# Reordering the opening loads and stores, the woven tiles' weight split and one prefix product in a fused spectral and expert kernel

## The chip, the cores and the metric

One core of one Trainium2 chip runs the whole program. The metric is the device time of one execution in microseconds. Three timed runs of the kernel before gave 1442.25 to 1444.67 us, with a median of 1443.52 us.

## What is computed

The input `x` has 8 batches of 2496 rows by 256 columns. Each batch is Fourier-transformed along its rows, mixed by a complex 256 by 256 weight, shrunk towards zero, and transformed back. Each of the 19968 rows then goes to the one of eight experts that its gate prefers.

```python
X = np.fft.rfft(x, axis=1)
Yr = Xr @ w_r - Xi @ w_i + b_r
Yi = Xr @ w_i + Xi @ w_r + b_i
Yr = np.sign(Yr) * np.maximum(np.abs(Yr) - 0.01, 0.0)
...
y = np.fft.irfft(Y, n=x.shape[1], axis=1)
...
logits = x @ w_gate
expert_idx = np.argmax(logits, axis=1)
...
h = np.maximum(xe @ w1[e], 0.0)
out[mask] = gate_w[mask, None] * (h @ w2[e])
```

## The kernel before, in words

The transform of 2496 = 39 x 64 points goes in two steps. The first (`fwd_a`, L367) multiplies the 39-point part and takes the input in six blocks per batch, `x(b, 0)` to `x(b, 5)`: five blocks of 117 rows (468 KB) and a last one of 78 rows (156 KB). `load_x` (L328) fetches a block. A block holds two pairs of columns `g = 0, 2`, the last one only `g = 0`, so a batch has eleven pairs and eleven products. What `fwd_a` makes is copied from PSUM to SBUF (`ae`, or for batch 0 the still unused tile `zs[1]`) and stored to a scratch tensor in HBM, `spec`, of 120 rows. The second step reads `spec` back, turned: `turn(b, s)` (L396) issues two loads of 128 KB each for slot `s` of ten slots, and slot `s` needs rows 12s to 12s+11 of all that was stored. I write t(n) for slot n counted over all batches, so t(10) is batch 1, slot 0.

For batches after the first, `round_x` (L356) makes on ScalarE (ACT) the rounded copy `xah` of a pair, and `rest_x` on GpSimd (POOL) makes its remainder. From batch 2 on `round_x` runs two iterations ahead of the product.

`spectral` (L582) is one order written by hand for TensorE (PE), VectorE (DVE), ACT and the DMA queue of SyncE (SP). After an opening for batch 0 alone it runs 80 iterations `it`, one per slot. Iteration `it` begins on PE with `fwd_b` of t(it+1), the products `pb` from `t` and the basis `bm`; then come `inv_b` (`pv`) of an earlier slot, `mix` (`pk`, `pm`), the `fwd_a` products of the next batch (`first`), and pieces of the batch before. ACT and DVE cut `pb` into `sh` and `sl` (`halves`, L420). `pb` has one PSUM buffer, so the next `fwd_b` waits until DVE's last read of it (`sl`, L430). At an iteration's end stand, in this order, `round_x` for two iterations on, the loads of the basis, the turns for five (at first) or four iterations on, and the loads of x blocks (`loads`).

SP issues its DMAs strictly in this order. A turn waits on SP until the stores of its rows have landed, and all that stands behind it on SP waits too. Basis `bm` comes in five pieces of 256 KB (`load_basis`); of the inverse basis `bi` three pieces are made by PE transposes and an ACT copy (`turn_basis`, L262), and two are loaded (`load_inverse`).

When the last batch has been transformed back, `finish_last` (L792) weaves the first seven expert tiles with the rest of the routing: after each step of a tile, `breathe` advances the queue of routing jobs. A tile t is `up` (hidden layer, products `ph`, L1137) and `down` (products `po`). Between the four quarters of `up`, `split2` (L1110) cuts the second half of a new expert's weights into `h2` under an `If` that holds only where the expert changes, and `upright` (L1119) prepares the next tile: a transpose, the rounding `xh` on ACT, the remainder `xl` on DVE. `route` (L833) yields "hold" ahead of its prefix product `pr` (L873), which keeps `tick` from going on until the next `breathe`.

Of the kernel before, what the change touches and what calls it, by code (L numbers as in the profile page):

```python
# [24 lines left out]
D = 256  # L25
# [84 lines left out]
class Kernel:  # L110
# [80 lines left out]
    def open_forward(self, st):  # L191
        tc, nc, nb = self.tc, self.nc, self.nb
        f = self.f = self.pool(st, "f", 1, side="right")
        self.xst = ExitStack()
        self.xp = self.pool(self.xst, "xp", 3)
        self.skip(self.xp, 224)
        self.xh, self.xl = {}, {}
        self.tp = self.pool(st, "tp", 6, side="right")
        self.w = self.pool(st, "w", 2, side="right")
        self.psf = self.pool(st, "psf", 1, side="right", space=PSUM)  # L200

        y = [self.w.tile([128, 2, D], F32, tag="y", name=f"first{i}", bufs=3) for i in range(2)]
        self.idle, self.row1, self.brow = y[0][:, 0, :].bitcast(BF16), y[0][0:1, 1, 0:128], y[1][0:1]
        nc.vector.memset(self.idle, 0.0)
        nc.vector.memset(self.row1, 1.0)
        far = f.tile([117, 240], F32, name="far")
        self.far, self.fer = far[:, 0:120], far[0:78, 120:240]
        nc.sync.dma_start(far, self.c_fa)
        self.bm = f.tile([128, K1, 128], F32, name="bm")
        self.bi = f.tile([128, K1, 128], F32, name="bi")  # L210
        self.bias = f.tile([128, 2, D], F32, name="bias")
        self.bias_r = f.tile([128, 2, D], F32R, name="bias_r")
        self.ones = f.tile([128, 128], F32R, name="ones")
        self.xg = {}
        for z, zf in zip(self.zs, self.zf):
            for c in range(2):
                nc.vector.memset(z[:, c, 64:66, :], 0.0)
            nc.vector.memset(zf[:, 5280:5288], 0.0)
        for q in range(6):
            self.load_x(0, q)  # L220
        raw = self.wi.tile([128, 4, D], F32, tag="yb", name="wraw", bufs=4)
        nc.sync.dma_start(raw, self.w_in.rearrange("(c p) n -> p c n", p=128))
        self.skip(self.wi, 160)
        self.raw = {"r": raw[:, 0:2, :], "i": raw[:, 2:4, :]}
        nc.sync.dma_start(self.brow, self.b_in.rearrange("(o h) n -> o h n", o=1))
        self.wh, self.wl = {}, {}
        for nm in "rds":
            self.wh[nm] = f.tile([128, 2, D], F32R, name="wh" + nm)
            self.wl[nm] = f.tile([128, 2, D], F32R, name="wl" + nm)
        self.nlam = f.tile([128, 1], F32, name="nlam")  # L230
        nc.vector.memset(self.nlam, -LAM)
# [138 lines left out]
    def fwd_a(self, b, q, g):  # L370
        nc = self.nc
        x = self.part_x(b, q, g)
        p = self.psi.tile([128, 512], F32, tag="u", name="pa", bufs=4)
        if b:
            h, l = self.xh.pop((b, q, g)), self.xl.pop((b, q, g))
            fh, fl = self.fhl[q == 5]
            for i, (a, v) in enumerate(((fh, h), (fl, h), (fh, l))):
                nc.tensor.matmul(p[:120, :], a, v, start=i == 0, stop=i == 2)
        else:
            nc.tensor.matmul(p[:120, :], (self.far if q < 5 else self.fer)[:x.shape[0], :], x, start=True, stop=True)  # L380
        n = 2 * q + g // 2 - 1
        if b or n < 0:
            ae = self.xp.tile([120, 2, D], F32, tag="ae", name="ae", bufs=4)
            to = ae.rearrange("p g d -> p (g d)")
        else:
            to = self.zs[1][:120, n // 5, 0:NB, :].rearrange("p n a -> p (n a)")[:, n % 5 * 512:n % 5 * 512 + 512]
            ae = to.rearrange("p (g d) -> p g d", g=2)
        if b == 0 and g:
            nc.vector.tensor_copy(to, p[:120, :])
        else:  # L390
            with self.tc.high_priority():
                nc.scalar.copy(to, p[:120, :])
        if b:
            nc.sync.dma_start(self.spec[b % 2][:, 4 * q + g:4 * q + g + 2, :], ae)
        elif n < 0:
            self.first_ae = ae  # L396
# [186 lines left out]
    def spectral(self, fwd):  # L583
# [5 lines left out]
        pairs = [(q, g) for q in range(6) for g in ((0, 2) if q < 5 else (0,))]  # L589
        todo = [(b, s) for b in range(nb) for s in range(10)]  # L590
        n = len(todo)
        self.keep_warm(10)
        nc = self.nc
        for i, pair in enumerate(pairs):
            self.fwd_a(0, *pair)
            if i in (0, 5):
                self.store_first(0, 48, *((-1, 0) if i == 0 else (0, 5)))
            if i == 5:
                self.load_basis(0, 4)
            if i in (8, 10):  # L600
                self.store_first(0, 32, *((5, 8) if i == 8 else (8, 10)))
        self.store_first(32, 48, 5, 10)
        self.turn(0, 0, (0,))
# [7 lines left out]
        self.load_basis(8, 12)  # L611
        if nb > 1:
            self.load_x(1, 1)
        self.store_rest(72, 120)
        self.load_basis(12, 16)
        self.keep_warm(6)
        self.spread_bias()
        self.keep_warm(6)
# [9 lines left out]
        for b in range(1, nb):  # L628
            at = 10 * b - 10
            for i, o in enumerate({1: (2, 2, 3, 3, 4, 4, 5, 5, 6, 6, 7), 2: (-2, -1, 0, 1, 1, 2, 3, 4, 4, 5, 6)}.get(  # L630
                    b, (-3, -2, -1, 0, 1, 2, 3, 3, 4, 5, 6))):
                first[at + o].append((b, *pairs[i]))
            for q, o in enumerate({1: (None, None, 0, 1, 2, 3), 2: (-5, -4, -3, -1, 0, 2)}.get(b, (-7, -5, -4, -2, 0, 2))):
                if o is not None:
                    loads[at + o].append((b, q))
        for b in range(nb):
# [4 lines left out]
        for b in range(nb - 1):  # L641
# [5 lines left out]
            for i in range(GH):  # L647
                o = i + 2 if i < 3 else i + 1
                (late if i == 3 else early)[at + o].append((self.inv_z, b, i))
                o = i + 3 if i < 3 else i + 2  # L650
                to = (late if i == 3 else early)[at + o]
                to.insert(0 if i == 2 else len(to), (self.inv_y, b, i))

        for it in range(n):
            b, s = todo[it]
# [53 lines left out]
            for a in first.get(it + 2, ()):  # L709
                if a[0] > 1:  # L710
                    self.round_x(*a)
            if it == 2:
                self.load_basis(16, 20)
            if it in (2, 4):
                self.turn_basis(it // 2)
            if it in (4, 6):
                self.load_inverse(*((12, 16), (16, 20))[it // 2 - 2])
            if not it:
                self.turn(*todo[4])
                self.turn(*todo[5])  # L720
            elif it < 5:
                self.turn(*todo[it + 5])
            for a in loads[it]:
                self.load_x(*a)
            if it in (2, 8, 9):
                self.load_tables(max(it - 7, 0), self.paced)
            if it == 6:
# [2 lines left out]
                self.split_bias(it - 7)  # L730
            if it == 11:
                self.write_blank(self.us[b, s][0:1, 0, 0:1])
            if 6 < it < n - 4:
                if it == 7:
                    self.turn(*todo[it + 3])
                self.turn(*todo[it + 4])
            if b == nb - 3 and s == 6:
                self.tabling = self.table(0)
            if b == nb - 1 and s == 2:
# [93 lines left out]
    def route(self, b, hf, y, gates):  # L833
# [35 lines left out]
        yield  # L869
        nc.vector.reciprocal(y[:, :, 0], sm)  # L870
        yield "hold"
        p = self.psi.tile([128, 512], F32, tag="yo", name="pr")
        nc.tensor.matmul(p[:117, :E], self.ltri, rank[:, :, GH - 1], start=True, stop=False)  # L873
        nc.tensor.matmul(p[:117, :E], self.ones_b[:, :117], self.carry_b, start=False, stop=True)
# [263 lines left out]
    def up(self, t, work=()):  # L1138
# [14 lines left out]
        for f2 in range(4):  # L1153
            if f2 % 2 and self.wide:
                p = self.psi.tile([128, 512], F32, tag="u", name="ph", bufs=4).rearrange("p (i t) -> p i t", i=2)
            else:
                p = (self.psb if self.psb and f2 % 2 else self.psa).tile([128, 2, TT], F32, tag="h", name="ph")
            for i in range(2):
                f = f2 * 2 + i
                m = 0  # L1160
                for c in range(2):
                    for a, v in ((h1, xh), (l1, xh), (h1, xl)):
                        nc.tensor.matmul(p[:, i, :], a[:, c, f * 128:(f + 1) * 128], v[:, c, :],  # L1163
                                         start=m == 0, stop=m == 5)
                        m += 1
            s = slice(f2 * 2, f2 * 2 + 2)
            with self.tc.high_priority():
                nc.scalar.activation(hh[:, s, :], p, AF.Relu)  # L1168
                nc.vector.scalar_tensor_tensor(out=hl[:, s, :], in0=p, scalar=0.0, in1=hh[:, s, :],  # L1169
                                               op0=ALU.max, op1=ALU.subtract)  # L1170
            next(work, None)
            if t and f2 % 2 == 0 and not self.psb:
                self.split2(t, (f2, f2 + 1))
            if t > 1 and f2 % 2:
                self.pace(hh.bitcast(F32)[0:1, f2 * 2, 0:1])
                self.send(1)
            yield
# [148 lines left out]
```

## Time and profile before

| what | value |
|---|---|
| median of three timed runs | 1443.52 us |
| the profiled execution: its own time | 1455.2 us |
| its span, first to last instruction | 1453.3 us |
| PE busy | 1429.0 us, 98% of the span |
| DVE, ACT, POOL busy | 64%, 53%, 34% of the span |
| bytes moved by DMA | 161.34 MB |

PE is busy nearly all the time, so what counts are the few stretches in which it is not. The profile gives for each instruction the idle time of its engine just ahead of it and what ended that time. A stretch's row gives the granted clock of PE (1.00 is 2.4 GHz, 0.50 is 1.2 GHz) and what the DMA engines moved.

### The profile page before, as it was taken

The numbers are of one execution on the slowest core, as the hardware profiler recorded it, in microseconds if no ns is written. First come the engines' busy times: TensorE is split into PE (matmuls) and PEld (weight loads), VectorE is DVE, ScalarE is ACT, GpSimd is POOL, SyncE is SP. The second block draws the span as 40 slices with busy tenths as digits, with TensorE's granted clock in tenths as the row PEclk, the third lists the DMA queues.
The fourth block names the chain that finished last, engine by engine and source line by source line (L and its number), as shares of the span: only waits on it lengthen the run. The fifth ranks groups of instructions, "written<-read, shape, count | busy, mean of one in ns | idle before, by whom it ended". The sixth has DMA issues, their size and how long they took to land. (4 is left out here: it accounts for less than half of the span.)

```text
span 1453.3 us, 35136 instructions
## 1 busy us (share of the span) xinstructions
PE 1429.0 (98%) x10521; PEld 1308.2 (90%) x10522; DVE 926.8 (64%) x1960; ACT 770.1 (53%) x1551; POOL 490.8 (34%) x595
## 2 busy tenths in 40 slices
PE   8999999999999989999999999999999999999998
PEld 5889898898989877899999999999999999999997
DVE  4788898988998875555555545454646445446444
ACT  4878787777877763443444434343435334335332
POOL 0452565766674454334311112112112112112111
PEclk9999999999999999999999999999999999999999
DMA  8774565565554232444343323242324224223220
GB/s 236 238 215 133 145 187 161 162 175 164 166 153 151 71 98 72 118 124 111 92 106 105 102 53 107 48 105 66 86 53 105 49 49 107 53 60 89 49 49 29
DMA packets 193212, 161.34 MB, mean 111 GB/s; under 512 B 127163, under 2 KB 163798, under 8 KB 192788
## 3 DMA queue, kind: packets, MB, share of 16 engines
q1 hardware_dynamic: 173043, 114.63, 31.1%
q0 software_dynamic: 19808, 44.03, 8.7%
q8 instruction: 94, 1.54, 0.5%
q14 instruction: 123, 1.00, 0.2%
q10 hardware_dynamic: 144, 0.13, 0.0%
HBM read 241.22 MB, written 66.37 MB: 212 GB/s over the span
## 5 line engine op out<-in xcount | busy, mean ns | idle before, releaser
L1163 PE MATMUL ph<-xh,l 128*128 128x256 f32 x1312 | 363.0, 277 | 0.2 <-DVE l L1094 0.2
L1163 PE MATMUL ph<-xh,h 128*128 128x256 f32 x1312 | 363.1, 277 | 0.0
L1163 PE MATMUL ph<-xl,h 128*128 128x256 f32 x1312 | 362.9, 277 | 0.0
L1203 PE MATMUL po<-h,hh 128*128 128x512 f32 x1296 | 310.5, 390 | 2.3 <-DVEq L1113 1.5
L1169 DVE SCALAR_TENSOR_TENSOR hl<-ph,hh 128x512 fp32r<-128x512 f32 x328 | 225.5, 688 | 134.7 <-ACT hh L1168 115.0
L1212 POOL DMA_INDIRECT out<-o,row x124 | 123.4, 995 | 551.6 <-DVE o L1210 521.3
L1168 ACT ACTIVATE hh<-ph 128x512 fp32r<-128x512 f32 x328 | 194.8, 600 | 189.0 <-PE ph L1163 160.6
L1203 PEld LDWEIGHTS po<-h,hh 128*128 128x128 f32 x1296 | 236.5, 188 | 48.9 <-ACTq L1105 2.9
L1210 DVE SCALAR_TENSOR_TENSOR o<-po,xr,part 128x256 f32<-128x256 f32 x156 | 74.0, 483 | 278.5 <-ACT part L1209 245.1
L1163 PEld LDWEIGHTS ph<-xh,l 128*128 128x128 f32 x1312 | 246.3, 188 | 0.6 <-DVE l L1094 0.4
L1163 PEld LDWEIGHTS ph<-xh,h 128*128 128x128 f32 x1312 | 246.3, 188 | 0.5 <-ACT yb L543 0.3
L1163 PEld LDWEIGHTS ph<-xl,h 128*128 128x128 f32 x1312 | 246.6, 188 | 0.0
L1209 ACT ACTIVATE part<-po,xr 128x256 f32<-128x256 f32 x156 | 72.3, 474 | 312.6 <-PE po L1205 279.0
L892 POOL DMA_INDIRECT xs_dram<-yb,pos x176 | 178.5, 1014 | 59.6 <-issue 47.9
L1205 PEld LDWEIGHTS po<-h,hl 128*128 128x128 f32 x1296 | 165.1, 188 | 6.9
L1205 PE MATMUL po<-h,hl 128*128 128x256 f32 x1296 | 167.3, 279 | 0.0
L483 DVE SCALAR_TENSOR_TENSOR y<-v,r 64x256 f32<-64x256 f32 x320 | 134.1, 419 | 5.8 <-ACT r L477 0.6
L366 POOL TENSOR_TENSOR xal<-x,xah 117x512 fp32r<-117x512 f32 (+1 forms) x77 | 97.4, 1270 | 0.2 <-issue 0.2
L831 POOL COPY mark<-y 1x1 f32<-1x1 f32 x77 | 27.4, 356 | 203.9 <-DVE y L483 168.7
L503 ACT COPY z<-pv 128x256 f32<-128x256 f32 x160 | 94.0, 709 | 0.5 <-PE py L536 0.5
L416 PE MATMUL pb<-bm,t 128*128 128x128 f32 x640 | 87.7, 280 | 6.0 <-DMA t<-spec_dram 6.0
L416 PEld LDWEIGHTS pb<-bm,t 128*128 128x128 f32 x640 | 79.0, 193 | 15.9 <-issue 9.9
(205 smaller groups left out, 2474.1 us busy)
## 6 DMA issues: line engine op xcount, KB each, us to landing
r<-moe_w SPq DMA_DIRECT2D x672, 128.0 KB
r<-moe_w SPq DMA_DIRECT2D x166, 512.0 KB
xq<-xs_dram SPq DMA_DIRECT2D x332, 64.0 KB
t<-spec_dram SPq DMA_DIRECT2D x159, 128.0 KB
spec_dram<-ae SPq DMA_DIRECT2D x77, 240.0 KB
x<-x SPq DMA_DIRECT2D x38, 468.0 KB
xs_dram<-yb,pos POOLq DMA_INDIRECT x176
xs_dram<-blank POOLq DMA_DIRECT2D x8, 264.0 KB
```

What stands on the lines that cost most here:

```text
L366: i = self.paced = self.nc.gpsimd.tensor_sub(l, x, self.xh[b, q, g])
L416: nc.tensor.matmul(p[:, c, :, kp, :], t[:, kp, c * 128:(c + 1) * 128], self.bm[:, 2 * s + kp, :], start=True, stop=True)
L483: nc.vector.scalar_tensor_tensor(out=y[q * 64:q * 64 + 64, kp, :], in0=u[h, q, :], scalar=LAM, in1=r[h, q, :], op0=ALU.add, op1=ALU.min)
L503: nc.scalar.copy(self.zs[b % 2][:, c, 0:NB, 4 * s:4 * s + 4].rearrange("p n a -> p a n"), p[:, c].rearrange("p a r n -> p (a r) n"))
L892: i = nc.gpsimd.indirect_dma_start(out=self.xs[:, :], out_offset=bass.IndirectOffsetOnAxis(ap=pos[:n, g:g + 1], axis=0), in_=y[:n, g, :], ...
L1163: nc.tensor.matmul(p[:, i, :], a[:, c, f * 128:(f + 1) * 128], v[:, c, :], start=m == 0, stop=m == 5)
L1168: nc.scalar.activation(hh[:, s, :], p, AF.Relu)
L1169: nc.vector.scalar_tensor_tensor(out=hl[:, s, :], in0=p, scalar=0.0, in1=hh[:, s, :], op0=ALU.max, op1=ALU.subtract)
L1203: nc.tensor.matmul(p, hh[:, f, hs], w2[:, f].rearrange("p a d -> p (a d)"), start=f == 0, stop=False)
L1205: nc.tensor.matmul(p[:, :D], hl[:, f, hs], w2[:, f, 0, :], start=False, stop=f == 7)
L1210: nc.vector.scalar_tensor_tensor(out=o[:, h, :], in0=p[:, :D], scalar=xr[:, h, 0:1], in1=part, op0=ALU.mult, op1=ALU.add)
L1212: i = nc.gpsimd.indirect_dma_start(out=self.out[:, :], out_offset=bass.IndirectOffsetOnAxis(ap=at[h], axis=0), in_=o[:, h, :], in_offset=N ...
```

## The change

- In the opening the small block `x(0, 5)` is loaded first, and its product is the first of eleven instead of the last. The last product is now that of pair (4, 2); ACT and DVE each copy half of it out.
- `store_rest(72, 120)` leaves the opening. Rows 72 to 95 are stored at the end of iteration 0 and rows 96 to 119 at the end of iteration 2. The basis pieces 12 to 15 and 16 to 19 move from the opening and iteration 2 to iterations 2 and 4.
- `turn_basis` 1 moves from iteration 2 to iteration 1. `load_inverse` (16, 20) moves from iteration 6 to 7.
- For batch 2 the blocks 1 and 2 are loaded one iteration later (7 and 8). From iteration 7 on, the turn stands ahead of the x load of its iteration.
- In the last half batch `route` yields "hold" twice, so `pr` comes a step later.
- In `up`, `split2` stands ahead of the step of `upright`.

```diff
-        for q in range(6):
+        for q in (5, 0, 1, 2, 3, 4):
             self.load_x(0, q)
...
-        if b == 0 and g:
+        if (b, q, g) == (0, 4, 2):
+            nc.scalar.copy(to[:, :D], p[:120, :D])
+            nc.vector.tensor_copy(to[:, D:], p[:120, D:])
+        elif b == 0 and g:
...
-        for i, pair in enumerate(pairs):
-            self.fwd_a(0, *pair)
+        for i in (10, *range(10)):
+            self.fwd_a(0, *pairs[i])
...
-            if i in (8, 10):
+            if i in (8, 9):
                 self.store_first(0, 32, *((5, 8) if i == 8 else (8, 10)))
...
-        self.store_rest(72, 120)
-        self.load_basis(12, 16)
...
-            for q, o in enumerate({1: (None, None, 0, 1, 2, 3), 2: (-5, -4, -3, -1, 0, 2)}.get(b, (-7, -5, -4, -2, 0, 2))):
+            for q, o in enumerate({1: (None, None, 0, 1, 2, 3), 2: (-5, -3, -2, -1, 0, 2)}.get(b, (-7, -5, -4, -2, 0, 2))):
...
-            if it == 2:
-                self.load_basis(16, 20)
+            if it in (1, 4):
+                self.turn_basis(1 + it // 4)
             if it in (2, 4):
-                self.turn_basis(it // 2)
-            if it in (4, 6):
-                self.load_inverse(*((12, 16), (16, 20))[it // 2 - 2])
+                self.load_basis(*((12, 16), (16, 20))[it // 2 - 1])
+            if it == 5:
+                self.load_inverse(12, 16)
...
+            if 6 < it < n - 4:
+                if it == 7:
+                    self.turn(*todo[it + 3])
+                self.turn(*todo[it + 4])
+            if it == 7:
+                self.load_inverse(16, 20)
             for a in loads[it]:
                 self.load_x(*a)
+            if it in (0, 2):
+                self.store_rest(*((72, 96), (96, 120))[it // 2])
...
-            if 6 < it < n - 4:
-                if it == 7:
-                    self.turn(*todo[it + 3])
-                self.turn(*todo[it + 4])
...
         yield "hold"
+        if b == self.nb - 1 and hf:
+            yield "hold"
...
-            next(work, None)
             if t and f2 % 2 == 0 and not self.psb:
                 self.split2(t, (f2, f2 + 1))
+            next(work, None)
```

The first place is SP's queue behind the load of `x(1, 1)` (here `x_229`, after the change `x_230`). The next x names are `x(1, 2)` and `x(1, 3)`; `t1_341`, `t1_344` are t(4) and t(5), then `t1_338`, `t1_341`; t(6) is `t1_404`, then `t1_410`; `ae` and `z1` are the stores of rows. Before:

```order
L337 DMA x_229<-x 117x1024
L246 DMA spec0_dram<-ae_173 48x512
L246 DMA spec0_dram<-z1_104 48x2560 x2
L257 DMA bm_128<-c_bm 128x512
L403 DMA t1_341<-spec0_dram 64x2x256 x2
L403 DMA t1_344<-spec0_dram 64x2x256 x2
L337 DMA x_347<-x 117x1024
L403 DMA t1_404<-spec0_dram 64x2x256 x2
L337 DMA x_407<-x 117x1024
```

With the change:

```order
L337 DMA x_230<-x 117x1024
L406 DMA t1_338<-spec0_dram 64x2x256 x2
L406 DMA t1_341<-spec0_dram 64x2x256 x2
L337 DMA x_344<-x 117x1024
L246 DMA spec0_dram<-ae_176 24x512
L246 DMA spec0_dram<-z1_104 24x2560 x2
L406 DMA t1_410<-spec0_dram 64x2x256 x2
L337 DMA x_413<-x 117x1024
```

Three stores and a basis piece no longer stand ahead of t(4) and t(5). The turn t(6) now stands right behind the stores whose rows it reads. The same pattern, three stores and a turn with two `ae` stores between, comes again at t(8).

The second place is SP's queue in iterations 5 to 8: `x_743`, `x_820` and `x_893` are x(2, 0), x(2, 1) and x(2, 2), `t1_896` and `t1_899` are t(10) and t(11), and the `ae` stores are those of batch 1, ending with its last, `ae_871`. Before:

```order
L337 DMA x_743<-x 117x1024
L394 DMA spec1_dram<-ae_788 120x512
L394 DMA spec1_dram<-ae_795 120x512
L260 DMA bi_129<-c_bi 128x512
L337 DMA x_820<-x 117x1024
L394 DMA spec1_dram<-ae_871 120x512
L337 DMA x_893<-x 117x1024
L403 DMA t1_896<-spec1_dram 64x2x256 x2
L403 DMA t1_899<-spec1_dram 64x2x256 x2
```

With the change (`x_747`, `x_901`, `x_972` are the blocks, `t1_894`, `t1_897` the turns, `ae_872` the last store):

```order
L337 DMA x_747<-x 117x1024
L397 DMA spec1_dram<-ae_792 120x512
L397 DMA spec1_dram<-ae_799 120x512
L397 DMA spec1_dram<-ae_872 120x512
L406 DMA t1_894<-spec1_dram 64x2x256 x2
L406 DMA t1_897<-spec1_dram 64x2x256 x2
L260 DMA bi_129<-c_bi 128x512
L337 DMA x_901<-x 117x1024
L397 DMA spec0_dram<-ae_947 120x512
L406 DMA t1_969<-spec1_dram 64x2x256 x2
L337 DMA x_972<-x 117x1024
```

The blocks x(2, 1) and x(2, 2) now stand behind the turns. ACT's own order is as before there: the casts `xah` from x(2, 0) and x(2, 1) stand at the ends of iterations 6 and 8, each ahead of the next iteration's `re` and `sh`.

The third place is DVE in the third and fourth quarter of woven tile 1. `hl` is that tile's hidden remainder, `xl` belongs to the next tile, the branch of `split2` stands around the two cuts `h<-r,h`, and the other rows are routing. Before:

```order
L1169 SCALAR_TENSOR_TENSOR hl<-ph,hh 128x512
L1135 TENSOR_TENSOR xl_8625<-xf,xh_8624 128x512
L1113 COMPARE_AND_BRANCH
L1100 TENSOR_TENSOR h_8045<-r_8023,h_8045 128x2x256 x2
L1113 UNCONDITIONAL_BRANCH x2
L856 SCALAR_TENSOR_TENSOR hot<-hot,score 117x88
L860 TENSOR_REDUCE mx<-hot 117x11
L862 SCALAR_TENSOR_TENSOR hot<-hot,mx 117x11x8
L1169 SCALAR_TENSOR_TENSOR hl<-ph,hh 128x512
```

With the change:

```order
L1176 SCALAR_TENSOR_TENSOR hl<-ph,hh 128x512
L1120 COMPARE_AND_BRANCH
L1107 TENSOR_TENSOR h_8049<-r_8027,h_8049 128x2x256 x2
L1120 UNCONDITIONAL_BRANCH x2
L1142 TENSOR_TENSOR xl_8629<-xf,xh_8628 128x512
L861 SCALAR_TENSOR_TENSOR hot<-hot,score 117x88
L865 TENSOR_REDUCE mx<-hot 117x11
L867 SCALAR_TENSOR_TENSOR hot<-hot,mx 117x11x8
L1176 SCALAR_TENSOR_TENSOR hl<-ph,hh 128x512
```

The branch passes `xl`; the last `hl` stands where it did.

## Rows read from the trace of the kernel before

**Rows 1.** Page, part 1: engines' busy time, share of the span, instructions.

```profile
PE 1429.0 (98%) x10521; PEld 1308.2 (90%) x10522; DVE 926.8 (64%) x1960; ACT 770.1 (53%) x1551; POOL 490.8 (34%) x595
```

**Rows 2.** Waits of PE, whole span: total us, times, longest us.

```profile
PE pb L416 <- DMA t<-spec_dram: 6.0, 4, 2.4
...
PE po L1203 <- DVE h L1100: 0.4, 1, 0.4
```

**Rows 3.** Timeline of PE, 34 to 56 us: start, length, instruction, [idle before].

```profile
34.19 0.71 PE L499 MATMUL pv<-bi,y 128*128 128x128 f32 x4 [0.65 <-DVE y L483]
...
38.48 0.60 PE L266 MATMUL pi<-ident,bm 128*128 128x128 f32 x4
41.45 2.05 PE L416 MATMUL pb<-bm,t 128*128 128x128 f32 x8 [2.38 <-DMA t<-spec_dram]
...
44.84 0.36 PE L449 MATMUL pk<-whr,sh 128*128 128x256 f32 x1
...
54.10 1.06 PE L416 MATMUL pb<-bm,t 128*128 128x128 f32 x8
...
55.80 0.37 PE L449 MATMUL pk<-whr,sh 128*128 128x256 f32 x1
```

**Rows 4.** Windows: engines' busy us, then PE clock, DMA share, GB/s.

```profile
36.00:58.00 22.00, 19.62 (x134) 18.05 (x133) 13.94 (x29) 16.66 (x36) 11.02 (x13) 0.92 0.87 264
42.00:44.00 2.00, 2.00 (x12) 2.00 (x11) 0.00 (x0) 0.41 (x2) 1.10 (x2) 0.50 0.98 256
46.00:52.00 6.00, 6.00 (x45) 5.55 (x44) 4.79 (x11) 5.17 (x12) 2.85 (x3) 1.00 1.01 329
```

**Rows 5.** Timeline of SP's DMA queue, 58 to 76 us.

```profile
59.43 0.35 SPq L337 DMA_DIRECT2D x<-x  x1
...
69.11 0.32 SPq L394 DMA_DIRECT2D spec_dram<-ae  x1
...
72.68 2.54 SPq L403 DMA_DIRECT2D t<-spec_dram  x4
```

**Rows 6.** Timeline of SP's DMA queue, 16 to 20 us.

```profile
16.77 0.77 SPq L246 DMA_DIRECT2D spec_dram<-z  x2
19.49 0.69 SPq L403 DMA_DIRECT2D t<-spec_dram  x1
```

**Rows 7.** Timeline of PE, 69 to 81 us: iterations 8, 9 and 10.

```profile
69.27 1.05 PE L416 MATMUL pb<-bm,t 128*128 128x128 f32 x8
...
76.10 1.13 PE L416 MATMUL pb<-bm,t 128*128 128x128 f32 x8 [1.89 <-DMA t<-spec_dram]
...
80.75 1.05 PE L416 MATMUL pb<-bm,t 128*128 128x128 f32 x8
```

**Rows 8.** Timeline of ACT, 64 to 75 us: ends of iterations 6 and 8.

```profile
64.14 1.16 ACT L359 CAST xah<-x 78x512 fp32r<-78x512 f32 x2
...
65.85 0.37 ACT L427 COPY re<-pb 128x256 f32<-128x256 f32 x1 [0.35 <-PE pb L416]
...
73.79 0.62 ACT L359 CAST xah<-x 117x512 fp32r<-117x512 f32 x1
74.44 0.62 ACT L314 CAST bh<-bias 1x512 fp32r<-1x512 f32 x1
```

**Rows 9.** Timeline of DVE, 67 us: last read of pb in iteration 7.

```profile
67.25 0.68 DVE L430 TENSOR_TENSOR sl<-pb,sh 128x512 fp32r<-128x512 f32 x1
```

**Rows 10.** Timeline of PE, 564 to 568 us: woven tile 1.

```profile
564.69 1.17 PE L1203 MATMUL po<-h,hh 128*128 128x512 f32 x4 [1.48 <-DVEq L1113]
566.35 0.17 PE L873 MATMUL pr<-rank,ltri 117*117 117x8 bf16 x1 [0.49 <-DVE rank L864]
...
567.45 2.02 PE L1203 MATMUL po<-h,hh 128*128 128x512 f32 x8
```

**Rows 11.** Timeline of DVE, 563 to 566 us: woven tile 1.

```profile
563.81 0.68 DVE L1135 TENSOR_TENSOR xl<-xf,xh 128x512 fp32r<-128x512 f32 x1
...
565.37 0.68 DVE L1169 SCALAR_TENSOR_TENSOR hl<-ph,hh 128x512 fp32r<-128x512 f32 x1
```

## The prediction

> **What bounds the kernel now.** I read the page's busy times first, then the waits of PE, then the timelines of the few places where PE waits. PE is busy 98% of the span [rows 1], so only its idle time, or a slower clock, can be won or lost. The waits of PE [rows 2] name the largest sum: four waits of `fwd_b` for its slot t, 6.0 us, all in the first 80 us. The longest, 2.38 us, is t(4) at 41.45 [rows 3]. It cost more than itself: right behind it PE's granted clock was 0.50, that is 1.2 GHz [rows 4], and from `pb` to `pk` it took 3.39 us (41.45 to 44.84), where iteration 5 took 1.70 (54.10 to 55.80) [rows 3]. The second, 1.89 us, is t(10) at 76.10 [rows 7]. Behind it stands a chain: the last store of batch 1 is issued at 69.11, the turn that reads it only at 72.68 [rows 5]. Far later, in woven tile 1, PE waits 1.48 us for DVE's branch of `split2` and 0.49 us for the prefix product [rows 10].
>
> The stretch between the two t waits shows a second bound. From 36 to 58 us the DMA share is 0.87 at 264 GB/s [rows 4]: the queue is hardly ever empty. What PE wins there by order alone it may have to give back to bytes.
>
> **The first products: nothing.** The first product follows the warm-up products and the last copy out, halved, ends about 0.2 us sooner; but the earlier stores come one product (some 0.86 us) later. t(0) waits for the store issued at 16.77 and is turned at 19.49 [rows 6]. I take 0, between -0.3 and +0.9.
>
> **t(4): 4.6 us won for a while.** Ahead of t(4) three stores (1056 KB) and a basis piece (256 KB) fall away; at 264 GB/s that is 5.1 us, more than the wait of 2.38. So the wait goes, and with it the slow clock: 3.39 - 1.70 = 1.69 us. `turn_basis` 1 leaves 38.48, just ahead of `fwd_b` of t(4), and moves to iteration 1, where PE next waits 0.65 us for DVE's `y` [rows 3]. That wait covers its 0.57 us (38.48 to 39.07); without it they would be paid there. Sum 2.38 + 1.69 + 0.55 = 4.6 us. From iteration 3 to 7 all of PE, DVE and ACT runs 4.6 us earlier.
>
> **Who is late next: x(2, 0).** ACT casts this block at the end of iteration 6, as the second of the pair that starts at 64.14, so at about 64.7 [rows 8]; now it would want it at 60.1. When does it land? The queue's order is fixed, so I count bytes. Before t(4) was through at 41.45, the stores, the basis piece and t(4) itself (1.61 MB) took 6.1 us; so x(1, 1) was through at about 35.3, and up to there SP's order is unchanged but for the first blocks. From there to x(2, 0) the changed queue holds twelve turn halves (1536 KB), four blocks (1872), the small block (156), the moved stores (1056), eight `ae` stores (1920), two basis pieces (512) and one inverse piece (256): 7.48 MB. At 264 GB/s that is 28.3 us: 63.6. At a full share (264/0.87 = 303) it is 24.7 us, plus two new pauses, since t(6) and t(8) wait on SP for stores just ahead of them with almost nothing behind: each some 2.3 us until data flows again (a turn's 2.8 us less its 0.5 us of data). That is 64.6. I take 64.0; the ends are 60.0 (303 GB/s, no pauses) and 68.2 (264 and both pauses in full).
>
> So ACT stands still from about 60.1 to 64.0, and iteration 7's `re` follows 1.15 us after the cast (64.7 to 65.85 [rows 8]), at 65.15. DVE's `sl` ends 2.08 us after `re` (67.93 against 65.85 [rows 9]); iteration 8 begins at 67.2 instead of 69.27 [rows 7]. Of 4.6 us there are 2.1 left.
>
> **t(10) and x(2, 1).** The last store of batch 1 is issued 3.26 us after that `re` (69.11 - 65.85): 68.4. No x load lies ahead of it now. From a store to the turn that waits for it the rows show 2.72 us [rows 6] and 3.57 with x blocks in the queue [rows 5]; I take 2.72, the nearer case: 71.1. PE had t(10) 3.42 us after its first issue (72.68 to 76.10): 74.5, or 1.6 us earlier than before. But x(2, 1) now stands behind four turn halves (2.54 us [rows 5]) and an inverse piece (0.4 us to issue): 74.05. A block lands 4.1 to 5.3 us after its issue (a half's 2.8 us with 1.8 us of data for its 0.5; or x(2, 0), issued at 59.43 and cast at 64.7 without a wait); I take 4.5: 78.55. ACT reaches that cast long before (73.79 in the kernel before [rows 8]) and everything of iteration 9 waits behind it on ACT. Cast and `bh` take 1.27 us, so `re` of iteration 9 runs at 79.8 and `fwd_b` of iteration 10 at 81.9, against 80.75 [rows 7]. That is 1.15 us **later** than before. Iteration 9 itself keeps PE busy 4.65 us (76.10 to 80.75), to 79.15, so PE idles 2.75 us. After 1.89 us idle the clock stayed [rows 7]; after 2.38 it fell and cost 1.69 [rows 3, 4]. The nearer row is the latter, so 1.7 us more. x(2, 2) is issued some 2 us behind and wanted an iteration later; it is hidden. The later blocks have two iterations or more, so the turned order of turn and load costs nothing there.
>
> Opening in sum: +1.15 + 1.7 = +2.85 us.
>
> **The woven tiles: 1.5 us won.** DVE's branch stands behind `xl` (0.68 us [rows 11]); now ahead of it, so PE goes on at 564.0 instead of 564.69. `pr` no longer stands in its way, so the narrow products start 1.17 us later at 565.2. The last two of eight need the last `hl`, whose place on DVE is unchanged: it ends at 566.05 [rows 11]. The group ends at 566.3 instead of 567.45 [rows 10]: 1.15 us. The same at the tile where the expert changes: 0.37 of the 0.4 us [rows 2], since `xl` is longer than that. `xl` itself is wanted a whole `down` later, so its delay is hidden; the table of tiles comes one step later and is read thirteen tiles on. Ends: 0 and 2.4 us (all three waits in full).
>
> **Sum.** +2.85 - 1.5 = +1.35 us. The profiled execution took 1455.2 us, 0.8% over the median of 1443.52; on a few us that is nothing, so I add to the median: 1444.9 us. A measurement of this kernel can tell about 0.2%, 2.9 us, from no change. The forecast lies inside.
>
> **Rivals.** *A, faster: the x blocks reach ACT in time.* Then iteration 8 begins at 64.7, t(10) is on PE at 70.65 and iteration 10 begins at 75.3, 5.45 us earlier; with the tiles 1436.6 us. If only x(2, 0) is in time, x(2, 1) is issued at 70.15, lands at 74.65 and iteration 10 begins at 78.0: 1439.3, or 1441.0 with a slow clock. For it: the queue held 329 GB/s from 46 to 52 us [rows 4], which without pauses lets x(2, 0) land at 58. Against it: 264 over the long stretch, and x(2, 1) behind four waiting turns. The Trainium skill (DMA: Bandwidth & Descriptors, Specifications) gives about 358 GB/s as a core's limit to HBM; by it the 7.48 MB take 20.9 us, x(2, 0) lands at 56.2, or 60.8 with the pauses, and the time is A's. The trace does not agree: no stretch here holds that rate. Chance 0.26.
>
> *B, slower: x(2, 0) lands late.* Every us of its landing passes through ACT, the store, t(10) and x(2, 1) to iteration 10. From 65.6 on the loss is over 2.9 us in all; at 66.5 it is +2.5 + 1.35 = +3.85, 1447.4 us. For it: both pauses in full. Against it: the rate of rows 4 already contains pauses. Chance 0.22.
>
> *C, the t(4) wait stays.* SP turns t(4) only when the stores of rows 48 to 71 have landed; if these are as late as t(4) is now, the opening gains and loses nothing: 1442.0 us. Against it: 5.1 us of bytes leave the queue ahead. Chance 0.10.
>
> **Numbers.** Forecast 0.42, C 0.10, both inside 0.2%: same 0.52. Faster 0.26 (A), slower 0.22 (B). The range runs from 1438.5, which leaves out A's far case, to 1448.0, which leaves out x(2, 0) later than 67.
>
> **What would show it.** Right: no wait of PE for t(4) and clock 1.00 there; ACT idle ahead of the cast of x(2, 0) and, for 3 us or more, of x(2, 1), released by a DMA; PE idle ahead of iterations 8, 9 and 10; the three DVE waits of the tiles shorter. Wrong: casts without a wait (A), or PE still waiting for t(4) (C).

## The result and the profile after

The changed kernel took 1455.97 us, the median of six runs (1453.74 to 1457.03). The kernel before took 1443.97 us beside it (1441.74 to 1445.87, six runs). The ratio is 1.0083, with a 95% interval from 1.0070 to 1.0096. The change is **slower by 12.0 us**; the forecast was +1.4 us, with a range up to +4.5.

The profiled execution took 1455.5 us, as the timed ones did. The page, part 1, and the waits of PE over the whole span (compare [rows 1, 2]):

```profile
PE 1429.7 (98%) x10521; PEld 1312.1 (90%) x10522; DVE 930.6 (64%) x1960; ACT 780.2 (54%) x1552; POOL 487.6 (34%) x595
```

```profile
PE pb L419 <- ACT r L480: 4.8, 1, 4.8
PE pa L378 <- ACT xah L359: 4.2, 1, 4.2
PE pb L419 <- DMA t<-spec_dram: 3.3, 3, 1.8
```

The busy shares tell nothing. The waits do: those for `t` fell from 6.0 to 3.3 us, and two waits for ACT, of 4.8 and 4.2 us, are new. The timeline of PE, 23 to 98 us, shows where they stand (compare [rows 3, 7]):

```profile
23.98 1.13 PE L419 MATMUL pb<-bm,t 128*128 128x128 f32 x8 [1.80 <-DMA t<-spec_dram]
...
39.50 1.05 PE L419 MATMUL pb<-bm,t 128*128 128x128 f32 x8
...
44.80 1.05 PE L419 MATMUL pb<-bm,t 128*128 128x128 f32 x8
...
51.67 0.78 PE L378 MATMUL pa<-xah,fah 117*120 117x512 f32 x1 [4.23 <-ACT xah L359]
...
58.29 1.17 PE L419 MATMUL pb<-bm,t 128*128 128x128 f32 x8
...
80.56 1.13 PE L419 MATMUL pb<-bm,t 128*128 128x128 f32 x8 [1.18 <-DMA t<-spec_dram]
...
90.17 2.05 PE L419 MATMUL pb<-bm,t 128*128 128x128 f32 x8 [4.79 <-ACT r L480]
...
97.64 0.60 PE L419 MATMUL pb<-bm,t 128*128 128x128 f32 x4
```

t(0) comes 1.0 us later (PE had it at 22.96 before). The wait for t(4) is gone: iteration 3 begins at 39.50 instead of 41.45. Two iterations on, at 58.29, PE is 4.2 us **behind** (54.10 before), and at 90.17 it is 9.4 us behind (80.75 before). Iteration 10 then takes 7.5 us, to 97.64 (4.6 before). The windows show why: engines' busy us, then PE's clock, DMA share and GB/s (compare [rows 4]):

```profile
40.00:44.00 4.00, 4.00 (x31) 3.70 (x31) 2.91 (x7) 3.24 (x7) 4.00 (x5) 1.00 0.39 146
...
52.00:58.00 6.00, 5.86 (x21) 4.57 (x21) 3.96 (x9) 4.89 (x11) 3.72 (x4) 0.50 0.66 228
89.50:95.50 6.00, 5.33 (x23) 5.26 (x24) 5.01 (x11) 5.94 (x14) 2.66 (x4) 0.50 0.40 105
```

Behind each of the two waits PE ran at 1.2 GHz. At that clock 6 us hold the work of 3 (in the kernel before there is one such stretch, from 41.43 to 44.84 by the trace's clock record). And from 40 to 44 us the DMA engines were busy 0.39 of the time, when SP had plenty to issue. Over the longer stretch of [rows 4] the queue moved 216 GB/s instead of 264:

```profile
36.00:58.00 22.00, 17.63 (x107) 15.25 (x106) 12.63 (x27) 13.52 (x28) 10.78 (x13) 0.86 0.71 216
```

ACT's timeline has the two places at which it stood:

```profile
43.29 0.59 ACT L395 COPY ae<-pa 120x512 f32<-120x512 f32 x1
50.51 0.58 ACT L395 COPY ae<-pa 120x512 f32<-120x512 f32 x1 [6.64 <-DMA spec_dram<-ae]
51.00 1.14 ACT L359 CAST xah<-x 117x512 fp32r<-117x512 f32 x2
...
78.50 0.58 ACT L395 COPY ae<-pa 120x512 f32<-120x512 f32 x1
86.87 0.62 ACT L359 CAST xah<-x 117x512 fp32r<-117x512 f32 x1 [7.79 <-DMA x<-x]
...
88.16 0.37 ACT L430 COPY re<-pb 128x256 f32<-128x256 f32 x1
```

The first waits for an `ae` buffer, 6.64 us, with the casts behind it that PE wants. The second waits for x(2, 1), 7.79 us, with iteration 9's `re` behind it. SP's queue tells why both came late:

```profile
36.59 0.37 SPq L246 DMA_DIRECT2D spec_dram<-ae  x1
37.01 0.77 SPq L246 DMA_DIRECT2D spec_dram<-z  x2
43.20 1.23 SPq L406 DMA_DIRECT2D t<-spec_dram  x2
44.53 0.50 SPq L337 DMA_DIRECT2D x<-x  x1
45.14 0.78 SPq L397 DMA_DIRECT2D spec_dram<-ae  x2
...
49.11 0.37 SPq L246 DMA_DIRECT2D spec_dram<-ae  x1
49.59 1.60 SPq L246 DMA_DIRECT2D spec_dram<-z  x2
52.45 1.47 SPq L397 DMA_DIRECT2D spec_dram<-ae  x2
57.23 1.23 SPq L406 DMA_DIRECT2D t<-spec_dram  x2
...
74.46 0.32 SPq L397 DMA_DIRECT2D spec_dram<-ae  x1
77.04 2.54 SPq L406 DMA_DIRECT2D t<-spec_dram  x4
79.62 0.60 SPq L260 DMA_DIRECT2D bi<-c_bi  x1
80.26 0.39 SPq L337 DMA_DIRECT2D x<-x  x1
```

The stores of rows 72 to 95 are out at 37.78, and the turn t(6), which reads them, is issued at 43.20: SP stood 5.4 us, and behind it x(1, 3) and the `ae` stores. SP's own waits, 0 to 110 us (total, times, longest), name the stores as what it waited for:

```profile
SPq L406 <- DMA spec_dram<-z: 13.0, 5, 5.3
```

The `ae` store of 45.14 landed at 50.4 by the trace's semaphore events, and that released ACT. There were four `ae` buffers, and one was still held by batch 0's first tile, whose last rows now leave only at 49.11. The second block, x(2, 1), was issued at 65.17 before (the row below is from the same view as [rows 5]), now at 80.26, behind four turn halves that wait for the last store of batch 1.

```profile
65.17 0.51 SPq L337 DMA_DIRECT2D x<-x  x1
```

### The profile page after: what moved, and what is told of

Read it like the earlier page. It is cut to its first block, busy times and chain, and to the rows that moved or that the text cites. A ratio compares the mean times of both kernels' runs of the same rounds, so it can differ in the third digit from the quotient of the medians.

```text
span 1453.7 us, 35134 instructions
## 1 busy us (share of the span) xinstructions
PE 1429.7 (98%) x10521; PEld 1312.1 (90%) x10522; DVE 930.6 (64%) x1960; ACT 780.2 (54%) x1552; POOL 487.6 (34%) x595
```

## The experiments

The kernels of each of the four groups below ran on one chip, beside the kernel before on that chip; ratios are to that. So between groups ratios are compared, not times.

**The kernel before again, and two stalls taken out one by one.** The theory was that two stalls of ACT are the whole loss. `e2` puts SP's order of iterations 6 to 8 back, `e3` gives the first `ae` tile a buffer of another pool, `e4` does both:

```diff
-            for q, o in enumerate({1: (None, None, 0, 1, 2, 3), 2: (-5, -3, -2, -1, 0, 2)}.get(b, (-7, -5, -4, -2, 0, 2))):
+            for q, o in enumerate({1: (None, None, 0, 1, 2, 3), 2: (-5, -4, -3, -1, 0, 2)}.get(b, (-7, -5, -4, -2, 0, 2))):
...
-            ae = self.xp.tile([120, 2, D], F32, tag="ae", name="ae", bufs=4)
+            ae = (self.xp if b else self.wi).tile([120, 2, D], F32, tag="ae" if b else "yb", name="ae", bufs=4)
```

In `e2` and `e4` the turns of iterations 7 on stand behind the x loads again, and `load_inverse` (16, 20) in iteration 6.

*e1, the kernel before again.*

> The kernel before, profiled once more. It is asked whether the first profile of it stood for its timed runs. Theory: no. That profile lasted 1455.2 us, the timed runs 1441.7 to 1445.9, and PE lost about 9.5 us in it between 460 and 600 us, behind DVE waits that the profile of the changed kernel does not show. A second profile then takes about 1444 us and has no waits of 1.48 and 0.49 us in woven tile 1; the opening is as on record (t(4) waits 2.4 us, the tenth iteration begins at 80.8). Rival: the waits of the woven tiles belong to the kernel; they are there again and the time is again near 1455.

It took 1456.7 us where the timed runs beside it had a median of 1450.2. The rival was right: the tile waits are there again, and this execution too lies above its timed runs, by 6.5 us. The wait for t(4) was longer than in the first profile, and PE's clock was 1.2 GHz for 6.8 us from 42.46 on:

```profile
43.34 2.04 PE L416 MATMUL pb<-bm,t 128*128 128x128 f32 x8 [3.75 <-DMA t<-spec_dram]
```

```profile
565.28 1.16 PE L1203 MATMUL po<-h,hh 128*128 128x512 f32 x4 [1.75 <-DVEq L1113]
566.93 0.17 PE L873 MATMUL pr<-rank,ltri 117*117 117x8 bf16 x1 [0.50 <-DVE rank L864]
```

*e2, x(2, 1) early.*

> The changed kernel with its queue of iterations 6 to 8 put back: x(2,1) and x(2,2) an iteration earlier and ahead of the turns. Theory (two stalls of ACT, each worth a wait of PE of over 4 us and some 3.4 us of half clock): the second stall goes, that is 4.8 us of PE waiting for ACT's re and 3.4 us of slow clock; the first (ACT waiting 6.6 us for an ae buffer) stays. Gain about 8 us, 1448 us. Rival (bytes): the queue is so full that an earlier issue brings x(2,1) no earlier by more than the change in its place; ACT still waits over 4 us, and the gain is under 3 us.

Ratio 1.0038 (1.0024 to 1.0051): 0.45% better than the change (1.0083 on the first chip), 6.5 us. ACT's wait for x is gone, that for the buffer (6.14 us at 49.21) stays.

*e3, the buffer of its own.*

> The changed kernel with the first ae tile of batch 0 in a buffer that nothing else wants then, so that its late stores hold no ae buffer of batch 1. Theory (two stalls): ACT's wait of 6.6 us at 50.5 goes, with PE's 4.2 us for xah and 3.4 us of half clock; then x(2,0) and x(2,1) are waited for instead, as predicted, and the second stall costs what it did or more. Gain 3 to 7 us, 1449 to 1453 us. Rival (the queue of SP itself, not the buffer, is behind: t(6) stands behind its stores): PE waits for t(6) or t(7) in place of ACT's buffer, and the gain is under 2 us.

Ratio 1.0093 (1.0077 to 1.0108): no gain at all. The first stall shrank (ACT waited 2.58 us for an `ae` store at 51.45 instead of 6.64, PE 2.35 us at 53.21), and ACT then stood for x(2, 0) as the prediction had said, but longer; its timeline:

```profile
72.24 0.62 ACT L359 CAST xah<-x 117x512 fp32r<-117x512 f32 x1 [6.68 <-DMA x<-x]
...
88.49 0.62 ACT L359 CAST xah<-x 117x512 fp32r<-117x512 f32 x1 [7.67 <-DMA x<-x]
```

*e4, both.*

> The changed kernel with both of the former edits: the first ae tile in a buffer of its own, and x(2,1) and x(2,2) early. Theory (two stalls are the whole loss): 14 to 16 us less than the changed kernel, 1440 to 1443 us, that is 1 to 4 less than before. Rival (a third cause: the small block first, the stores late, or the woven tiles): over 1446 us, with a loss against before that these two stalls don't hold.

Ratio 1.0050 (1.0036 to 1.0064), so the theory fell: with both named causes gone, a loss remains. ACT's wait for x(2, 0) took their place:

```profile
70.03 0.62 ACT L359 CAST xah<-x 117x512 fp32r<-117x512 f32 x1 [6.04 <-DMA x<-x]
```

SP's queue points to the blocked turns, t(6) at 42.07 and t(8) at 56.03, as the cause behind both; `e7` and `e8` test it:

```profile
35.96 0.77 SPq L246 DMA_DIRECT2D spec_dram<-z  x2
42.07 1.23 SPq L406 DMA_DIRECT2D t<-spec_dram  x2
...
56.03 1.23 SPq L406 DMA_DIRECT2D t<-spec_dram  x2
...
62.52 1.03 SPq L337 DMA_DIRECT2D x<-x  x1
```

x(2, 0) went out at 62.52, 3.1 us later than in the kernel before (59.43 [rows 5]), though PE began iteration 6 sooner (57.82 against 59.40). A basis piece came late too: PE waited 2.40 us for t(6)'s products, to 52.44; that piece had just landed (52.35 by the semaphore events).

**The parts one by one, and turns that aren't blocked.** The new theory: SP stands behind turns that directly follow their own stores. `e7` is `e2` with the stores and basis pieces back in the opening. `e8` is `e4` with the stores moved away from the turns that read them:

```diff
             if not it:
                 self.turn(*todo[4])
                 self.turn(*todo[5])
-            elif it < 5:
-                self.turn(*todo[it + 5])
+                self.store_rest(72, 96)
...
             for a in loads[it]:
                 self.load_x(*a)
-            if it in (0, 2):
-                self.store_rest(*((72, 96), (96, 120))[it // 2])
+            if it == 1:
+                self.store_rest(96, 120)
+            if 0 < it < 5:
+                self.turn(*todo[it + 5])
```

*e5, the kernel before with the two tile edits.*

> The kernel before with the two edits of the woven tiles alone (split2 ahead of the next tile's xl, the last prefix product a step later). Theory of the prediction: 1.5 us less than before (between 0 and 2.4), a ratio of 0.998 to 1.000; the three waits for DVE (1.75, 0.50 and 0.38 us in the second profile of before) are shorter. Rival: the step that goes later is itself late somewhere (the tables, the tile that reads them), and the ratio is 1.001 or more.

Ratio 0.9983 (0.9972 to 0.9994): **2.5 us won**, as forecast within its ends. This run also showed a wait for t(4) behind which the clock stayed at 1.00:

```profile
40.97 1.13 PE L416 MATMUL pb<-bm,t 128*128 128x128 f32 x8 [2.54 <-DMA t<-spec_dram]
```

```profile
40.00:44.00 4.00, 3.03 (x24) 2.97 (x25) 0.92 (x2) 1.81 (x5) 2.50 (x4) 1.00 0.86 234
```

In woven tile 1 the waits for the branch and for the prefix product are gone. The third, at the tile where the expert changes, did not get shorter as forecast: it is 0.62 us here and in the changed kernel, 0.37 before.

*e6, the first products.*

> The kernel before with the opening's product order alone (the small block first, its product first, the last copy halved). Prediction: 0 us, between -0.3 and +0.9. Theory from the profile after (the first fwd_b came 1.0 us later there, 23.98 against 22.96): a ratio of 1.000 to 1.001. Rival: the later start is the stores' turn on the queue of that chip alone, and the halved copy wins: 0.9995 or less.

Ratio 1.0010 (0.9997 to 1.0024). Its first `fwd_b` stood at 23.73, against 22.28 in `e5` on the same chip.

*e7, the stores back.*

> The changed kernel with x(2,1) and x(2,2) early and, besides, the stores of rows 72 to 119 and the basis pieces back in the opening, ahead of t(4); the ae tile is as in the changed kernel. What is left of the change is the small block first, turn_basis 1 an iteration earlier and the woven tiles. Theory (SP stands blocked at t(6) and t(8) behind their own stores for over 5 us each, and the late ae tile and the late x(2,0) both follow from that): the rest of the loss goes, a ratio of 0.998 to 1.001; the wait for t(4) is there again, PE idles for nothing else in the opening over 2 us. Rival (the small block first or turn_basis costs it): the ratio stays at 1.003 or more.

Ratio 1.0009 (0.9996 to 1.0022), against 1.0038 of `e2`: the rest of the loss goes with the stores and basis pieces. The wait for t(4) is back (4.06 us).

*e8, no blocked turn.*

> A version meant to keep what the later stores win: as the kernel with the ae tile of its own and x(2,1) early, but the stores of rows 72 to 95 go out between t(5) and x(1,2), those of rows 96 to 119 one iteration earlier, behind x(1,3), and in iterations 1 to 4 the x blocks stand ahead of the turns, so that no turn follows its own store at once. Theory (the loss is SP blocked, not the bytes): no turn is issued more than 2 us after the DMA ahead of it on SP between 36 and 60 us, x(2,0) is issued before 58 us and ACT does not wait for it by over 2 us, the wait for t(4) stays away, and the ratio is 0.996 to 0.999. Rival (bytes: the queue moves 1.2 to 2 MB less than it would have to between 36 and 70 us): x(2,0) lands after 66 us all the same, PE idles over 3 us ahead of iteration 7 or 8, and the ratio is 1.003 or more.

Ratio 0.9996 (0.9986 to 1.0006), between the two. No turn stood behind its store and t(4) wasn't waited for; but x(2, 0) went out at 58.96, not before 58, and ACT waited 2.36 us for it, so bytes matter too. This is 0.54% better than `e4`, which differs only in where the stores and turns stand (the stores also go out earlier). ACT's row, and the window from 36 to 58 us:

```profile
65.46 0.62 ACT L359 CAST xah<-x 117x512 fp32r<-117x512 f32 x1 [2.36 <-DMA x<-x]
```

```profile
36.00:58.00 22.00, 20.92 (x155) 19.22 (x156) 17.16 (x36) 18.68 (x39) 12.94 (x15) 1.00 0.87 263
```

The queue moves 263 GB/s again, as in the kernel before (264 [rows 4]); `e4` had 213 and the changed kernel 216. So the lower rate goes with the blocked turns.

**The causes alone, and a version to keep.** `e9` is `e8` with the opening's products as before and the inverse piece of iteration 5 behind x(2, 0); `e12` is `e9` without the extra buffer. `e10` and `e11` are the kernel before with one part of the change each.

> The kernel before with one edit alone: x(2,1) and x(2,2) an iteration later and behind the turns, the inverse piece with them. Theory (ACT stands still for x(2,1), PE idles over 4 us ahead of iteration 10 and runs at half clock behind it): 6 to 9 us more than before, a ratio of 1.004 to 1.006, with ACT's wait for x of over 5 us at 80 to 90 us. Rival (the stall needs the delays of the later stores as well): t(10) comes earlier by having no x block ahead of it, the block lands within 3 us of its use, and the ratio is 0.999 to 1.002.

*e10:* ratio **1.0041** (1.0028 to 1.0055). ACT waited 7.12 us for x(2, 1), and PE stood:

```profile
82.11 2.05 PE L416 MATMUL pb<-bm,t 128*128 128x128 f32 x8 [4.36 <-ACT r L477]
```

The rival was wrong: the stall needs no help from the late stores.

> The kernel before with the stores of rows 72 to 119, their basis pieces and turn_basis 1 moved as in the change, and nothing else. Theory (SP blocked behind t(6) and t(8), and an ae buffer held): PE does not wait for t(4), ACT waits over 5 us for an ae store at about 50 us, PE idles some 4 us and runs at half clock behind that; 3 to 6 us more than before, a ratio of 1.002 to 1.004. Rival (the late stores cost only together with the small block first or the late x blocks): a ratio of 0.998 to 1.001.

*e11:* ratio **1.0025** (1.0016 to 1.0033). No wait for t(4), and in its place:

```profile
48.25 0.59 ACT L392 COPY ae<-pa 120x512 f32<-120x512 f32 x1 [6.58 <-DMA spec_dram<-ae]
```

```profile
49.40 0.55 PE L378 MATMUL pa<-xah,fah 117*120 117x512 f32 x1 [4.16 <-ACT xah L359]
```

> The version without blocked turns, with the opening's products in the order of the kernel before (its small block last) and the inverse piece of iteration 5 behind x(2,0) in place of ahead of it. Theory (the small block first costs about 1.5 us, the later stores win what the wait for t(4) costs once SP is not blocked): no wait for t(4), no half clock, x(2,0) waited for by less than 2 us, and 2 to 5 us less than before, a ratio of 0.9965 to 0.9985; better than the tiles alone (0.9983) or equal. Rival: the wait for t(4) costs the timed runs less than the profile shows, so that its going is worth nothing: the ratio is that of the tiles alone or above it, 0.998 to 1.000.

*e9:* ratio 0.9982 (0.9971 to 0.9994), in the band of both: better than before, no better than the tiles alone.

> The version without blocked turns and with the old opening once more, with the first ae tile of batch 0 back in the four ae buffers. Theory (the buffer matters only where its last store is late; here that store goes out at about 40 us and lands by 47): no more than 1 us over the version with a buffer of its own. Rival (four buffers are too few as soon as the first one is held past 40 us): ACT waits over 2 us for an ae store, and the ratio is higher by 0.002 or more.

*e12:* ratio **0.9972** (0.9961 to 0.9983), 1441.0 us against 1444.9: the fastest here, though not told apart from `e9`. ACT did wait 3.03 us for a buffer, as the rival said, but PE then stood only 0.68 us for the cast, and the time did not rise.

**What was still open: do the late parts add?**

> The kernel before with the late stores and the late x blocks, and without the woven tiles and the first products of the change. Theory (the two stalls stand one behind the other and add): the product of the two alone, 1.0066, between 1.005 and 1.008. Rival (they feed each other: the first stall delays the last ae store of batch 1, and so t(10) and the block behind it): 1.009 or more.

*e13:* ratio 1.0073 (1.0061 to 1.0085). The two alone multiply to 1.0066, so they add; no feeding of each other is seen.

> The kernel before with the small block and its product first, and the last copy out whole on DVE, as in the kernel before, in place of halved. Theory (the halves go one behind the other, 0.37 and 0.42 us, so the halving wins nothing, and the loss is the block's place): as with the halved copy, 1.000 to 1.0015. Rival (the halved copy, which waits for two engines, is the loss): 0.9985 to 1.000.

*e14:* ratio 1.0009 (0.9999 to 1.0019), as with the halved copy. So the halving is not the loss. What loss there is (this interval and that of `e6` both hold 1) goes with the block's place.

> The changed kernel once more, on the chip of the two others. Theory: the parts multiply, and this is the kernel with both late parts times 0.9993 (tiles and first products), near 1.006 to 1.0075. Rival (as on its first chip): 1.0083, more than the parts hold.

*e15:* ratio 1.0082 (1.0069 to 1.0095), as at first. `e13` times tiles and first products gives 1.0066. The 0.0016 between (2.3 us) is no more than the intervals leave, and stays **open**.

## Why the prediction was wrong

**In short:** a chain of stalls was foreseen in kind, but the later stores, which were to win 2.1 us by iteration 8, cost 3.6. A turn that stands behind its own store stops SP, a buffer was overlooked, and the rate of the queue was taken as if it held such stops already.

| part | forecast, us | alone, us |
|---|---|---|
| first products | 0 | +1.4 (`e6`) |
| later stores, up to iteration 8 | -2.1 | +3.6 (`e11`) |
| late x(2, 1), with the slow clock | +4.95 | +5.9 (`e10`) |
| woven tiles | -1.5 | -2.5 (`e5`) |
| sum | +1.35 | +8.5 (before rounding) |

The whole change measured +12.0 us. The forecast of the third part is made of the 2.1 us that were to be lost again, the 1.15 us behind and the 1.7 us of slow clock.

- **"From iteration 3 to 7 all of PE, DVE and ACT runs 4.6 us earlier": the step that failed first.** PE was 1.95 us early at iteration 3 and 3.6 us at iteration 4 (44.80 against 48.41), but 4.2 us late at iteration 5. The working named no resource that the moved store still held. The first tile of batch 0 held one of four `ae` buffers until its last rows were out, and ACT stood 6.64 us. `e11` shows it with the late stores and their basis pieces alone.
- **"Two new pauses ... each some 2.3 us": right for the data, but counted in the wrong place.** The data did pause about as long as that (in `e4` 2.4 us from the store's landing to the turn's first data, by the semaphore events). But SP waits until the store has *landed*, behind all that is queued ahead of it: 5.4 us at t(6) and, behind the `ae` stores of 52.45, 3.3 us at t(8). All that while nothing that stands behind is issued, the `ae` stores too, whose landing frees ACT's buffers. And the 64.0 for x(2, 0) lay between 264 GB/s without the pauses and 303 with them; as rival B has it, "the rate of rows 4 already contains pauses". It did not contain these: 216 GB/s with them, 263 without (`e8`). The pauses come on top of 264, which is the forecast's far end, 68.2; the cast stood at 70.50 in the changed kernel and at 70.03 in `e4`.
- **The rate itself.** The Trainium skill (DMA: Bandwidth & Descriptors, Specifications) gives about 358 GB/s as a core's limit. Two microseconds of the kernel before read more, 377:

```profile
46.00:48.00 2.00, 2.00 (x15) 1.75 (x14) 1.92 (x5) 1.87 (x5) 0.00 (x0) 1.00 1.03 377
```

Over 6 us no run has more than 349 GB/s (the changed kernel, 110.25 to 116.25 us). So the prediction's "no stretch here holds that rate" is true of longer stretches only. The rate of a full queue was not the fault; the queue was not full.
- **t(4): right, but worth less than counted.** The wait and the half clock behind it are gone in the profile. But the half clock is not there each time: the profiles of `e5`, `e6` and `e10` have waits of 2.54, 2.45 and 3.17 us for t(4) with the clock at 1.00. So 1.69 of the 4.6 us was not there to be won each time. The timed runs agree as far as they can: in the 35 executions of the kernel before beside `e5` the mean clock lay between 0.996 and 1.000. Where in the run it fell is not recorded for them.
- **x(2, 0): the right block, undersized, and hidden.** In the changed kernel ACT came late to it by the stall ahead and waited only 1.41 us (2.15 in `e15`). With that stall removed or shrunk it stands as forecast, but for 6.0 to 6.7 us instead of 3.9 (`e4`, `e3`).
- **t(10) and x(2, 1): the right mechanism, somewhat too small.** "A block lands 4.1 to 5.3 us after its issue": here it was cast 6.6 us after it (80.26 to 86.87), behind four turn halves and a basis piece issued in the 3.2 us ahead of it. PE idled 4.79 us, not 2.75, and the half clock lasted 6.8 us, not 3.4 (in `e15` it did last 3.4). By itself the part costs 5.9 us (`e10`, 0.41%) where the forecast had 4.95.
- **First products: 0 was too good.** The stores of the first rows come 1.0 to 1.2 us later, about as the working said ("one product"), and t(0) with them. That "the last copy out, halved, ends about 0.2 us sooner" was wrong; the timeline of ACT and DVE in the changed kernel:

```profile
16.51 0.37 ACT L389 COPY z<-pa 120x256 f32<-120x256 f32 x1 [0.27 <-PE pa L380]
...
16.91 0.42 DVE L390 COPY z<-pa 120x256 f32<-120x256 f32 x1 [1.62 <-ACT z L389]
```

DVE's half waited for ACT's. From 16.51 to 17.33 the copy takes 0.82 us; whole on ACT, in the kernel before, it took 0.59. The part alone gives +1.4 us, with an interval that just holds 0.
- **The tiles: right in sum.** 1.5 us forecast, 2.5 measured (0.9 to 4.1). Two of the three waits went; the third, counted as 0.37 us won, grew by 0.25.
- **The signs of being right** came nearly all, though the time was wrong: no wait for t(4), ACT idle ahead of x(2, 0) and x(2, 1), PE idle ahead of iterations 9 and 10. None of them asked where PE stands at iteration 5.
- **Rivals.** B, the loss, was in kind what happened: x blocks late, ACT standing, PE's clock down. It had 0.22. Its point of decision, x(2, 0) after 65.6, did come (70.50), but the 4.2 us lost by then stood already at iteration 5 and came through the buffer, which B did not name. The parts measured alone make 0.9983 x 1.0010 x 1.0025 x 1.0041 = 1.0059, 8.5 of the 12.0 us; the other 3.5 are about as wide as the intervals, and stay open.

## What to carry to other kernels

Moving a store later moves three things: the bytes, the release of the tile it reads, and, if its reader stands close behind on the same queue, the issue of everything after that reader. Put independent loads between a store and the DMA that waits for it, and send the store early (`e8` against `e4`: 0.54%, both together). A new pause comes on top of a rate that was read without it. When a wait on a tuned kernel's path is removed, ask for each in-order engine what it waits for next, and price a load at its slowest row while the queue is full, not at its fastest.

## What the runs showed that was not expected

- After a wait of similar length the clock did not always do the same: it fell behind 2.38 us (before), 3.75 (`e1`) and 4.06 (`e7`) for t(4), and stayed at 1.00 behind 2.45, 2.54 and 3.17. It fell behind one of 2.35 in `e3` (at 53.21) and stayed behind one of 2.40 in `e4` (at 52.44). All PE's waits for ACT of 3.75 us and more were followed by 0.50. In `e8` it fell for 3.4 us behind a wait of 1.89 for t(0). And in `e12` it fell behind two waits of 0.68 and 0.63 us (0.67 in the mean from 48 to 52 us). What decides was not tried.
- One stretch differs by chip, whatever the kernel. From the `pv` near 457 us to the last `po` wait near 600, `e9` to `e12`, on the chip where the kernel before took 1444.9 us, needed 134.5 to 135.6 us; all eleven others, on the three chips where it took 1450.2 to 1451.5, needed 140.3 to 144.0. The profile of before needed 144.05 and that of the change 134.50. So the 0.8% (11.7 us) by which the profiled execution of before stood over its timed runs came largely from that stretch, if the timed runs had it as short as `e10` and `e11`, 135.6 us: that would be 8.4 us. It is not shown, since no trace of them was kept. The prediction called the 0.8% nothing, which did no harm, as it added to the median. Why chips differ there was not looked for.
